# Batch 1's loads reordered between those of w_out, its q copies all on ScalarE, its k^T v moved to slot 27, and its last x slot turned inside block 1: one cosformer attention and MoE kernel on one core

## The chip, the cores and the metric

The kernel runs on 1 core of a Trainium2 chip. The metric is device time in microseconds (us), as the median of several executions; lower is better. Each execution is listed with its span and the mean clock that TensorE was granted (1.0 is full speed).

## The reference

Attention with a cosine weighting of positions and no softmax, on 8 batches of 8 heads, 576 positions and 64 columns, then a feed-forward layer on the 4608 rows that come out.

```python
def phi(x, c, s):
    r = np.maximum(x, 0.0)
    return np.concatenate([r * c, r * s], axis=-1)        # 128 features
q_p, k_p = phi(q, cos_w, sin_w), phi(k, cos_w, sin_w)
kv  = np.einsum('bhsf,bhsd->bhfd', k_p, v)                # "k^T v"
z   = np.sum(k_p, axis=2)
num = np.einsum('bhsf,bhfd->bhsd', q_p, kv)
den = np.einsum('bhsf,bhf->bhs', q_p, z)[..., None] + 1e-06
x   = (num / den).transpose(0, 2, 1, 3).reshape(4608, 512)
h   = x @ w_in                                            # 512 x 2048
out = (h * (1.0 / (1.0 + np.exp(-1.702 * h)))) @ w_out    # 2048 x 512
```

## The kernel before

The feed-forward layer goes in 9 blocks of 512 rows. A block has 32 slots. Slots 0 to 15 each multiply x by one group of 128 w_in columns (`mm1`: 4 matmuls and a gelu on ScalarE); slots 16 to 31 each do 4 of the 64 w_out matmuls (`mm2`). Behind a slot, the attention work of the next batch is set by a table of (slot, work). Block 0 is special: batch 1's loads come late there, so TensorE's attention work for it is crowded into slots 22 to 31.

For batch 1 that work is: VectorE makes q and k features (`prep`) and copies v (`prep_v_wide`); TensorE turns q, four slots of 128 positions with 8 heads each (`turn_q_at`, out of PSUM by a copy); `unit_kv` is k^T v (48 matmuls, then two casts on VectorE); `unit_num` is a numerator (8 matmuls, then the division on VectorE, giving xb); `turn_x_at` turns xb into xT (4 transposes and a copy on ScalarE). In PSUM the kernel keeps four tiles `mm` of 512 float32 columns, and two tiles `at` of twice that, which q turns, k^T v, numerators and x turns share. `evac` copies a finished w_out result out of PSUM into the tile `ysb`, on ScalarE.

```python
    load_w_out(0)
    load_w_out(1)
    for n in "qkv":
        load_main(1, n)
    load_w_out(2)
    load_w_out(3)
    ...
    def turn_q_at(b, c, copy):
        t = at_tile()[:, 0].bitcast(BF16)...
        for h in range(H):
            nc.tensor.transpose(t[:, h], qn_slot(b, c)[:, h, :], ident[:rows(c), :rows(c)])
        copy(q_slot(b, c)[:, :, 0:rows(c)], t)
    ...
    def unit_kv(b):
        kvs_new(b)
        kv = at_tile()
        for n in range(2):
            kv_half(b, n, kv[:, n])       # 24 matmuls
        for n in range(2):
            kvs_half(b, n, kv[:, n])      # cast on VectorE
    ...
    for i in range(NBLK):
        ...
            k0, k1, ks = (11, 24, (25, 26, 27, 28)) if i == 0 else (0, 12, (17, 19, 21, 23, 25))
            ...
            for c in range(4 if i == 0 else NC):
                at(k0, prep, b, "q", c)
                if i == 0:
                    at(22 + c // 2, turn_q_at, b, c, VE.tensor_copy if c % 2 else AC.copy)
            for c in range(6 if b < 2 else NC):
                at(20 if i == 0 else k1 - 4 + c // 2, prep, b, "k", c)
            if b == 1:
                at(21, prep_v_wide, b)
            at(k1, unit_kv, b)
            for c, k in enumerate(ks):
                at(k, unit_num, b, c)
                if i == 0 and c < 4:
                    at(min(k + 2, 31), turn_x_at, b, c)
```

`AC` is ScalarE, `VE` is VectorE; `at(n, ...)` sets work behind slot n. Cuts are marked with "...".

Of the kernel before, what the change touches and what calls it, by code (L numbers as in the profile page):

```python
# [21 lines left out]
def kernel(  # L22
# [15 lines left out]
    TB = 512  # L38
# [15 lines left out]
    def rows(c):  # L54
        return 128 if c < 4 else 64

    def wide(b, n):
        return b < 2 and n != "q"
# [7 lines left out]
    def mm_tile():  # L66
        return ps.tile([128, TB], F32, name="mm", bufs=4)

    def at_tile():
        return ps.tile([128, 2, 512], F32, name="at", bufs=2)  # L70
# [10 lines left out]
    def load_main(b, n, h0=0, h1=H, on=nc.gpsimd):  # L81
        t = 6 if wide(b, n) else 4
        np_ = 96 if wide(b, n) else 128
        if h0 == 0:
            state[b][n] = two.tile([128, 2048 if n == "q" else 49 * D], BF16, name=n)
        on.dma_start(out=state[b][n][:np_, t * D * h0:t * D * h1].rearrange("p (h e) -> p h e", h=h1 - h0),  # L86
                     in_=SRC[n][b, h0:h1, 0:np_ * t, :].rearrange("h (p c) d -> p h (c d)", c=t))

    def load_tail(b, n, on=nc.gpsimd):
        if on is nc.gpsimd:  # L90
            t = two.tile([64, 512], BF16, name=n + "t")
        else:
            t = one.tile([64, 512], F32, name=f"{n}t{b}")
        state[b][n, 4] = t
        on.dma_start(out=t.rearrange("p (h d) -> p h d", h=H),
                            in_=SRC[n][b, :, 512:576, :].rearrange("h p d -> p h d"))
# [14 lines left out]
    def load_w_out(g):  # L111
        nc.gpsimd.dma_start(out=w_out_sb[:, ts(g, 4), :], in_=wout_r[:, ts(g, 4), :])
# [23 lines left out]
    load_w_in(3)  # L136
    load_w_out(0)
    load_w_out(1)
    for n in "qkv":
        load_main(1, n)  # L140
    load_w_out(2)
    load_w_out(3)
    load_tail(1, "q")
    load_all(2)
# [84 lines left out]
    def turn_x_at(b, c):  # L229
        t = at_tile()[:, 0].bitcast(BF16).rearrange("p (j t) -> p j t", j=2 * KC)[:, 0:KC, 0:rows(c)]  # L230
        for j in range(KC):
            nc.tensor.transpose(t[:, j], state[b]["xb"][:rows(c), c, 2 * j:2 * j + 2, :].rearrange("p h d -> p (h d)"),
                                ident[:rows(c), :rows(c)])
        nc.scalar.copy(xT[:, :, ds(b * S + c * 128, rows(c))], t)
# [45 lines left out]
    def mm1_part(hps, i, fc, c0=0, c1=TB):  # L280
        for kc in range(KC):
            nc.tensor.matmul(hps[:, c0:c1], w_in_sb[:, kc, ds(fc * 128, 128)], xT[:, kc, ds(i * TB + c0, c1 - c0)],  # L282
                             start=(kc == 0), stop=(kc == KC - 1))

    def gelu(hps, fc):
        g = gpool.tile([128, TB], BF16, name="g")
        nc.scalar.activation(g, hps, AF.Gelu_apprx_sigmoid)  # L287
        gT[fc] = g

    def mm1(i, fc):  # L290
        hps = mm_tile()
        if (i, fc) == (1, 0):

            mm1_part(hps, i, fc, 0, 448)
            mm1_part(hps, i, fc, 448, TB)
        else:
            mm1_part(hps, i, fc)
        gelu(hps, fc)

    def pieces(m):  # L300

# [20 lines left out]
    def mm2(i, t, part):  # L322

        if part == 0:
            cur[t] = mm_tile()
        yps = cur[t]
        for fc in range(part * 4, part * 4 + 4):
            nc.tensor.matmul(yps, gT[fc][:, ds(t * 128, 128)], w_out_sb[:, fc, :],  # L328
                             start=(fc == 0), stop=(fc == FC - 1))
        if part == 3 and (i > 0 or t < 3):  # L330
            evac(i, t)

    def evac(i, t, on=None):
        ysb = ypool.tile([128, d_model], F32, name="ysb")
        if on is nc.vector:
            nc.vector.tensor_copy(ysb, cur[t])
        else:
            nc.scalar.copy(ysb, cur[t])  # L338
        for (p0, n, row, step) in pieces(i * 4 + t):
            nc.gpsimd.dma_start(out=out[row:row + (n - 1) * step + 1:step, :], in_=ysb[p0:p0 + n, :])  # L340

    def mm2_last(i, t):

        yps = mm_tile()
        ysb = ypool.tile([128, d_model], F32, name="ysb")
        hd = d_model // 2
        for n in range(2):
            cols = ds(n * hd, hd)
            if n == 1:
                yps = mm_tile()  # L350
            for fc in range(FC):
                nc.tensor.matmul(yps[:, 0:hd], gT[fc][:, ds(t * 128, 128)], w_out_sb[:, fc, cols],  # L352
                                 start=(fc == 0), stop=(fc == FC - 1))
            if n == 0:
                nc.scalar.copy(ysb[:, cols], yps[:, 0:hd])
            else:
                nc.vector.tensor_copy(ysb[:, cols], yps[:, 0:hd])  # L357
            for m, (p0, cnt, row, step) in enumerate(pieces(i * 4 + t)):
                (nc.sync if m == 0 else nc.scalar).dma_start(out=out[row:row + (cnt - 1) * step + 1:step, cols],
                                                             in_=ysb[p0:p0 + cnt, cols])  # L360
# [57 lines left out]
    AC, VE = nc.scalar, nc.vector  # L418
# [50 lines left out]
    for i in range(NBLK):  # L469
        work = {n: [] for n in range(32)}  # L470
        b = i + 1

        def at(n, f, *a):
            work[n].append(lambda: f(*a))

        if b < B:
            if i == 0:
                at(18, unit_num, 0, 4)
                at(18, turn_x, 0, 4)
            k0, k1, ks = (11, 24, (25, 26, 27, 28)) if i == 0 else (0, 12, (17, 19, 21, 23, 25))  # L480
            at(k0, prep_new, b)
            if i == 1:

                at(2, nc.vector.memset, kp[64:128, 4], 0.0)
                at(2, nc.vector.memset, vt[64:128, 4], 0.0)

                at(0, prep, 1, "q", 4)
                at(0, turn_q, 1, 4)
                at(14, unit_num, 1, 4)
                at(14, turn_x, 1, 4)  # L490
            for c in range(4 if i == 0 else NC):
                at(k0, prep, b, "q", c)
                if i == 0:
                    at(22 + c // 2, turn_q_at, b, c, VE.tensor_copy if c % 2 else AC.copy)
                else:
                    at(k0 + c, turn_q, b, c)
            for c in range(6 if b < 2 else NC):
                at(20 if i == 0 else k1 - 4 + c // 2, prep, b, "k", c)
                if b >= 2:
                    at(k1 - 1, prep_v, b, c)  # L500
            if b == 1:
                at(21, prep_v_wide, b)
            at(k1, unit_kv, b)
            for c, k in enumerate(ks):
                at(k, unit_num, b, c)
                if i == 0 and c < 4:
                    at(min(k + 2, 31), turn_x_at, b, c)
                else:
                    at(k, turn_x, b, c)
            if i == 1:  # L510
                at(8, gate, 7)
            if 0 < i and b + 1 < B:
                at(8 if i == 1 else 1, load_all, b + 1)
        for n in range(32):
            if n < FC:
                if i > 0 or n > 2:
                    mm1(i, n)
            elif i == 0:
                mm2(i, n % 4, (n - FC) // 4)
            elif i == NBLK - 1 and n >= 28:  # L520
                if n == 28:
                    mm2_last(i, 3)
            else:
                mm2(i, (n - FC) // 4, n % 4)
            for f in work[n]:
                f()
        if i == 0:
            evac(i, 3, nc.vector)
# [30 lines left out]
```

## Time and profile before

| | us |
|---|---|
| median of the first 3 timed executions | 295.51 (295.04 to 295.58) |
| the profiled execution | 297.05, span 295.0, mean clock 0.994 |

The execution whose trace is read in the prediction took 1.5 us longer than any of the timed ones, and its clock was below 1. A stretch of 3.41 us at half clock takes about 0.006 off the mean clock of such a span (3.41 × 0.5 / 295), which is the gap between 1.0 and 0.994. The lines of the profiled execution's trace are in the prediction; each shows times in us from the start of the span.

### The profile page before, as it was taken

How to read it: one execution, taken by the hardware profiler on the slowest of the kernel's cores; microseconds unless marked ns; L12 is line 12 of the kernel's file. 1: busy time of each engine (PE TensorE's matmuls, PEld its weight loads, DVE VectorE, ACT ScalarE, POOL GpSimd, SP SyncE). 2: the span in 40 equal slices, each digit the busy share in tenths (PEclk: the TensorE clock that was granted, in tenths of full speed). 3: DMA queues.
4: the chain of work that ended last, by engine and by line, in shares of the span. 5: the costliest groups of instructions: out<-in, count | busy, mean ns of one | idle time of the engine just before them, and what ended most of it. 6: DMA issues, size and time to landing. Idle time of an engine off the chain costs nothing.

```text
span 295.0 us, 5044 instructions
## 1 busy us (share of the span) xinstructions
PE 285.0 (97%) x1920; PEld 144.9 (49%) x1956; DVE 106.1 (36%) x359; ACT 124.1 (42%) x212; POOL 96.2 (33%) x118
## 2 busy tenths in 40 slices
PE   8999969999999999999999999999999999999994
PEld 3654446545544554455445544554455444444443
DVE  5940475663580259015901581148114200000000
ACT  7866221673136313741264126511651176126411
POOL 8543340352277026602690268005401200120021
PEclk9999989999999999999999999999999999999999
DMA  7999999799989956998899779966904500011033
GB/s 188 189 203 200 203 198 192 186 148 180 194 160 182 169 118 118 191 155 136 155 181 185 107 140 174 190 110 124 185 1 71 118 36 3 36 71 36 2 71 71
DMA packets 87304, 39.65 MB, mean 134 GB/s; under 512 B 57137, under 2 KB 85041, under 8 KB 87281
## 3 DMA queue, kind: packets, MB, share of 16 engines
q0 software_dynamic: 40848, 27.01, 59.4%
q1 hardware_dynamic: 46272, 12.20, 25.0%
q8 instruction: 15, 0.25, 0.3%
q10 hardware_dynamic: 160, 0.13, 0.2%
q14 instruction: 9, 0.07, 0.1%
HBM read 36.70 MB, written 9.44 MB: 156 GB/s over the span
## 4 chain that ended last, share of the span: by engine, by line
PE 82%; DMA 9%; DVE 4%; POOL 1%; issue 1%; ACT 1%; ACTq 0%; DVEq 0%; POOLq 0%
PE mm L328 37%; PE mm L282 36%; DMA q<-in_q_dram 6%; PE at L266 3%; PE at L245 3%; DMA w_in_sb<-in_moe_w_in_dram 3%; PE mm L352 1%; DVE kp L207 1%; ACT g L287 1%; DVE xb L274 1%; DVE qn L207 1%; POOL v L86 1%; POOL k L86 0%; DVE vt L210 0%; DVE inv L273 0%
## 5 line engine op out<-in xcount | busy, mean ns | idle before, releaser
L328 PE MATMUL mm<-w_out_sb,g 128*128 128x512 bf16 x542 | 127.2, 380 | 0.9 <-issue 0.2
L282 PE MATMUL mm<-xT,w_in_sb 128*128 128x512 bf16 (+1 forms) x552 | 123.5, 377 | 0.8
L287 ACT ACTIVATE g<-mm 128x512 bf16<-128x512 f32 x144 | 85.6, 597 | 46.0 <-PE mm L282 45.5
L340 POOL DMA_DIRECT2D out_dram<-ysb x54 | 50.6, 941 | 166.1 <-ACT ysb L338 164.7
L282 PEld LDWEIGHTS <-w_in_sb 128*128 128x128 bf16 x568 | 54.8, 98 | 64.8
L328 PEld LDWEIGHTS <-g 128*128 128x128 bf16 x560 | 52.3, 98 | 57.1 <-issue 0.6
L338 ACT COPY ysb<-mm 128x512 f32<-128x512 f32 x34 | 19.9, 585 | 97.7 <-PE mm L328 97.7
L249 DVE CAST kvs<-at 128x260 bf16<-128x260 f32 x14 | 5.4, 426 | 58.4 <-PE at L245 58.4
L274 DVE TENSOR_TENSOR xb<-at,inv 128x512 bf16<-128x512 f32 (+1 forms) x36 | 24.8, 690 | 1.2
L357 DVE COPY ysb<-mm 128x256 f32<-128x256 f32 x1 | 0.4, 424 | 59.4 <-PE mm L352 59.4
L272 DVE TENSOR_SCALAR den<-at 128x8 f32<-128x8 f32 (+1 forms) x36 | 5.9, 164 | 43.8 <-PE at L266 43.8
L266 PEld LDWEIGHTS <-qT 128*128 128x128 bf16 x272 | 13.0, 98 | 8.2 <-DVE xb L274 0.6
L207 DVE TENSOR_SCALAR qn<-q,cosw 128x512 bf16<-128x512 bf16 (+1 forms) x36 | 12.4, 351 | 12.2 <-DMA q<-in_q_dram 12.2
L266 PE MATMUL at<-kvs,qT 128*128 128x65 bf16 x272 | 14.2, 194 | 0.5
L207 DVE TENSOR_SCALAR qn<-q,sinw 128x512 bf16<-128x512 bf16 (+1 forms) x33 | 11.9, 360 | 0.0
L245 PEld LDWEIGHTS <-kp 128*128 128x128 bf16 (+1 forms) x288 | 10.4, 101 | 2.0 <-issue 0.6
L86 POOL DMA_DIRECT2D v<-in_v_dram x10 | 9.8, 986 | 4.6 <-DMA v<-in_v_dram 2.4
L245 PE MATMUL at<-vt,kp 128*128 128x65 bf16 (+1 forms) x288 | 10.5, 198 | 0.0
L86 POOL DMA_DIRECT2D k<-in_k_dram x9 | 7.8, 863 | 3.0 <-DMA q<-in_q_dram 2.3
L207 DVE TENSOR_SCALAR kp<-k,cosw 128x512 bf16<-128x512 bf16 x24 | 8.2, 341 | 0.0
L207 DVE TENSOR_SCALAR kp<-k,sinw 128x512 bf16<-128x512 bf16 x24 | 8.2, 341 | 0.0
L273 DVE RECIPROCAL inv<-den 128x8 f32<-128x8 f32 (+1 forms) x36 | 7.2, 201 | 1.2
(78 smaller groups left out, 133.7 us busy)
## 6 DMA issues: line engine op xcount, KB each, us to landing
out_dram<-ysb POOLq DMA_DIRECT2D x38, 128.0 KB, 3.0
out_dram<-ysb POOLq DMA_DIRECT2D x16, 256.0 KB, 2.7
q<-in_q_dram POOLq DMA_DIRECT2D x7, 512.0 KB, 9.2
k<-in_k_dram POOLq DMA_DIRECT2D x6, 512.0 KB, 10.5
v<-in_v_dram POOLq DMA_DIRECT2D x6, 512.0 KB, 12.3
w_out_sb<-in_moe_w_out_dram POOLq DMA_DIRECT2D x4, 512.0 KB, 18.3
w_in_sb<-in_moe_w_in_dram POOLq DMA_DIRECT2D x3, 512.0 KB, 12.2
q<-in_q_dram SPq DMA_DIRECT2D x2, 512.0 KB, 4.2
```

Of the source, the lines that this page charges most:

```text
L86: on.dma_start(out=state[b][n][:np_, t * D * h0:t * D * h1].rearrange("p (h e) -> p h e", h=h1 - h0), in_=SRC[n][b, h0:h1, 0:np_ * t, :].r ...
L207: nc.vector.tensor_scalar(oc, i, 0.0, wc, op0=MAX, op1=MUL)
L245: nc.tensor.matmul(kv[:, ds(h % 4 * (D + 1), D + 1)], kp[:r, c, h, :], vt[:r, c, h, 0:D + 1], start=(c == 0), stop=(c == last))
L266: nc.tensor.matmul(nm[:, h // 4, ds(h % 4 * (D + 1), D + 1)], q_slot(b, c)[:, h, :], state[b]["kvs"][:, h // 4, h % 4, 0:D + 1], start=Tru ...
L272: nc.vector.tensor_scalar(den[:r], nm4[:, :, :, D], 1e-6, None, op0=ADD)
L273: nc.vector.reciprocal(inv[:r], den[:r])
L274: nc.vector.tensor_tensor(state[b]["xb"][:r, c].rearrange("p (n h) d -> p n h d", n=2), nm4[:, :, :, 0:D], inv[:r].unsqueeze(3).to_broadca ...
L282: nc.tensor.matmul(hps[:, c0:c1], w_in_sb[:, kc, ds(fc * 128, 128)], xT[:, kc, ds(i * TB + c0, c1 - c0)], start=(kc == 0), stop=(kc == KC ...
L287: nc.scalar.activation(g, hps, AF.Gelu_apprx_sigmoid)
L328: nc.tensor.matmul(yps, gT[fc][:, ds(t * 128, 128)], w_out_sb[:, fc, :], start=(fc == 0), stop=(fc == FC - 1))
L338: nc.scalar.copy(ysb, cur[t])
L340: nc.gpsimd.dma_start(out=out[row:row + (n - 1) * step + 1:step, :], in_=ysb[p0:p0 + n, :])
```

## The change: intent and diff

Batch 1's q is loaded first, then a part of w_out, so that w_out arrives before TensorE needs it; v comes in two halves, so that k^T v can start on the first. All q copies go to ScalarE, one turn per slot, which takes TensorE's wait on VectorE away. k^T v goes from behind slot 24 to behind slot 27, the numerators follow, and the last x slot is turned inside block 1, between two w_in groups that first do only the 448 columns that don't need it.

```diff
--- before.py
+++ after.py
@@ -136,9 +136,11 @@
     load_w_in(3)
     load_w_out(0)
     load_w_out(1)
-    for n in "qkv":
-        load_main(1, n)
+    load_main(1, "q")
     load_w_out(2)
+    load_main(1, "k")
+    load_main(1, "v", 0, 4)
+    load_main(1, "v", 4, 8)
     load_w_out(3)
     load_tail(1, "q")
     load_all(2)
@@ -288,14 +290,19 @@
         gT[fc] = g
 
     def mm1(i, fc):
-        hps = mm_tile()
         if (i, fc) == (1, 0):
 
-            mm1_part(hps, i, fc, 0, 448)
-            mm1_part(hps, i, fc, 448, TB)
-        else:
+            hps = [mm_tile(), mm_tile()]
+            mm1_part(hps[0], i, 0, 0, 448)
+            turn_x_at(1, 3)
+            mm1_part(hps[1], i, 1, 0, 448)
+            for f in range(2):
+                mm1_part(hps[f], i, f, 448, TB)
+                gelu(hps[f], f)
+        elif (i, fc) != (1, 1):
+            hps = mm_tile()
             mm1_part(hps, i, fc)
-        gelu(hps, fc)
+            gelu(hps, fc)
 
     def pieces(m):
 
@@ -477,7 +484,7 @@
             if i == 0:
                 at(18, unit_num, 0, 4)
                 at(18, turn_x, 0, 4)
-            k0, k1, ks = (11, 24, (25, 26, 27, 28)) if i == 0 else (0, 12, (17, 19, 21, 23, 25))
+            k0, k1, ks = (11, 27, (27, 27, 28, 29)) if i == 0 else (0, 12, (17, 19, 21, 23, 25))
             at(k0, prep_new, b)
             if i == 1:
 
@@ -491,20 +498,22 @@
             for c in range(4 if i == 0 else NC):
                 at(k0, prep, b, "q", c)
                 if i == 0:
-                    at(22 + c // 2, turn_q_at, b, c, VE.tensor_copy if c % 2 else AC.copy)
+                    at(23 + c, turn_q_at, b, c, AC.copy)
                 else:
                     at(k0 + c, turn_q, b, c)
             for c in range(6 if b < 2 else NC):
-                at(20 if i == 0 else k1 - 4 + c // 2, prep, b, "k", c)
+                at(24 if i == 0 else k1 - 4 + c // 2, prep, b, "k", c)
                 if b >= 2:
                     at(k1 - 1, prep_v, b, c)
             if b == 1:
-                at(21, prep_v_wide, b)
+                for n in range(2):
+                    at(26, prep_v_wide, b, 4 * n, 4 * n + 4)
             at(k1, unit_kv, b)
             for c, k in enumerate(ks):
                 at(k, unit_num, b, c)
-                if i == 0 and c < 4:
-                    at(min(k + 2, 31), turn_x_at, b, c)
+                if i == 0:
+                    if c < 3:
+                        at(28 + c, turn_x_at, b, c)
                 else:
                     at(k, turn_x, b, c)
             if i == 1:
```

## The prediction

> **What bounds the kernel now.** I read the page first (busy shares, then the chain that ended last), then the waits of TensorE, then the timeline and the windows of the stretch that those point to.
>
> The first two lines below are the page's busy line and its chain; the third is the longest wait in the list of TensorE's waits after the start.
>
> ```profile
> PE 285.0 (97%) x1920; PEld 144.9 (49%) x1956; DVE 106.1 (36%) x359; ACT 124.1 (42%) x212; POOL 96.2 (33%) x118
> PE 82%; DMA 9%; DVE 4%; POOL 1%; issue 1%; ACT 1%; ACTq 0%; DVEq 0%; POOLq 0%
> PE at L226 <- DVE qT L227: 2.1, 1, 2.1
> ```
>
> TensorE is busy for 285.0 of 295.0 us, so only some 10 us can be idle at all, and one single wait of 2.1 us stands out. It lies in the turn from block 0 to block 1. The chain of work there, in order of time (start, us, what):
>
> ```profile
> 14.55 18.46 DMA q<-in_q_dram
> ...
> 33.53 2.56 DVE qn L207 x8
> ...
> 36.42 0.68 DVE xb L274
> 37.10 3.15 DVE kp L207 x12
> 40.25 0.87 DVE vt L210
> 41.12 0.61 DVE qT L227
> ...
> 41.77 0.71 PE at L226 x8
> ```
>
> VectorE gets batch 1's q at 33.5, makes the q features, then the 12 k features and the whole v copy, and only then the copy of a turned q slot out of PSUM, which TensorE needs before it can use that PSUM tile again. The timeline of the same stretch (start, us, engine, line, operation, count, idle time before it):
>
> ```profile
> 39.03 0.61 PE L226 MATMUL at<-ident,qn 128*128 128x128 bf16 x8
> 39.73 1.01 ACT L227 COPY qT<-at 128x1024 bf16<-128x1024 bf16 x1 [0.75 <-PE at L226]
> 40.17 0.95 DVE L210 COPY vt<-v 96x3072 bf16<-96x3072 bf16 x1
> 41.77 0.71 PE L226 MATMUL at<-ident,qn 128*128 128x128 bf16 x8 [2.14 <-DVE qT L227]
> 43.99 2.32 PE L245 MATMUL at<-vt,kp 96*128 96x65 bf16 x48
> 46.35 0.77 DVE L249 CAST kvs<-at 128x260 bf16<-128x260 f32 x2 [3.13 <-PE at L245]
> 49.79 0.31 PEld L266 LDWEIGHTS <-qT 128*128 128x128 bf16 x8 [0.31 <-DVE xb L274]
> 51.44 0.31 PEld L266 LDWEIGHTS <-qT 128*128 128x128 bf16 x8 [0.31 <-DVE xb L274]
> 56.69 0.60 ACT L287 ACTIVATE g<-mm 128x512 bf16<-128x512 f32 x1 [0.27 <-PE mm L282]
> ```
>
> TensorE stands from 39.64 to 41.77. Then the granted clock falls, as two windows of 2 us show (column PEclk, third from the end of each line):
>
> ```profile
> 42.00:44.00 2.00, 1.78 (x11) 0.88 (x10) 0.69 (x1) 0.00 (x0) 0.28 (x1) 0.53 1.57 185
> 44.00:46.00 2.00, 2.00 (x45) 2.00 (x44) 0.00 (x0) 0.00 (x0) 0.00 (x0) 0.61 1.57 192
> ```
>
> The trace's clock records put half speed at 42.14 to 45.55. So one wait costs twice.
>
> **The ceiling of any gain here.** Two fixed points: slot 22 of block 0 ends at 37.26 (start of the first q turn), and the second w_in group of block 1 ends at about 56.47 (its gelu starts at 56.69, and starts after matmul issue ends by 0.2). That is 19.21 us. The work between, at the full-clock spacings seen elsewhere in this trace: 9 slots of 4 matmuls at 0.216 = 7.78; 4 q turns of 8 at 0.45 (16 took 0.90 from 37.26 to 38.16) = 1.80; k^T v, 48 at 0.030 (block 1's 40 took 1.21) = 1.45; 4 numerators at 0.26 = 1.04; 4 x turns at 0.22 = 0.88; two w_in groups = 1.73. Sum 14.7. Hence 4.5 us are lost: 2.14 in the wait, about 1.6 to half clock (the slot at 42.28 to 43.99 took 1.71 instead of 0.86, k^T v 2.15 instead of 1.45), 0.62 in two waits on xb, the rest small. 4.5 us is 1.5% of 295.5: even a perfect change stays inside 2%.
>
> [...] the q copy on VectorE started at 41.04 though its turn was done at 39.64; the v copy of 0.95 us stood ahead. [...]
>
> **The change part by part.**
>
> *Loads.* Before, the landings (completion records) are q 33.01, k 35.77, v 38.65, third w_out 41.16, fourth 44.15: 2.5 to 3.0 us each, back to back. With w_out moved up: third w_out at 33.01 + 2.51 = 35.5, k at 38.3, the halves of v at 39.7 and 41.2, last w_out at 44.1 as before. The w_out loads are needed only at slots 24 and 28 (38.6 and 46.2 below): both in time. k is 2.5 us later.
>
> *Copies of q.* All four q copies go to ScalarE (1.01 each, idle there), one per slot. Turn q0 follows slot 23: 37.26 + 0.86 = 38.12 to 38.57, copy 38.83 to 39.84; slot 24 to 39.43; q1 to 39.88; slot 25 to 40.74; q2 may begin, since copy q0 ended at 39.84. q2 to 41.19, slot 26 to 42.05, q3 to 42.50, slot 27 to 43.36. No wait: the 2.14 and the half clock behind it go.
>
> *k^T v at slot 27.* VectorE: k at 38.3 plus 0.5 (q landed at 33.01 and its first feature began at 33.53) = 38.8; 12 features 3.15 → 41.95; v halves at about 0.5 each → 42.45 and 42.9. TensorE arrives at 43.36: slack 0.9. k^T v to 44.81. So far TensorE is 1.3 us ahead of before (46.12).
>
> *Numerators right behind it.* Here a wait comes in. Before, slot 25 stood between k^T v and its use; now nothing does. The casts start when all 48 are done, 44.81 + 0.2, and take 0.77 → 45.78; numerator 0 ends at 45.96 instead of 45.07, numerator 1 at 46.21. Loss 0.9. Slot 28 to 47.08. The x product takes 1.13 (0.17 + 0.20 + 0.69 and gaps): xb0 at 47.29, so x turn 0 runs 47.32 to 47.55 (loss 0.24).
>
> *One PSUM tile.* In the built program numerator 2 takes the tile of x turn 0, so it waits for ScalarE's copy of it, which queues behind the ysb copy of slot 28: 47.29 to 47.87, the x copy to 48.37. Numerator 2 at 48.41 (loss 0.86) to 48.67; slot 29 to 49.53; x turn 1 to 49.75; xb2 at 50.0, so numerator 3 at 50.02 (0.27) to 50.28; slot 30 to 51.14; x turn 2 to 51.36; slot 31 to 52.22.
>
> *Block 1.* The first w_in group waits for the copy of x turn 2, which stands behind a ysb copy: 52.43, so 52.47 (0.25). Its 448 columns take 0.76, x turn 3 0.22, the second group's 448 columns 0.76 → 54.21. The x3 copy ended by 54.25, so the last 64 columns of both, 8 at 0.03, end at 54.54. The split adds four matmuls net, about 0.05 us.
>
> Sum: 56.47 − 54.54 = 1.9 us gained: 4.5 of old losses removed, about 2.6 of new ones put in. Later blocks start earlier with the same order; batch 2's loads keep their times and have 5 us or more. So 295.5 − 1.9 = 293.6.
>
> **Rivals.**
> *The clock halves again.* The new waits cluster from 44.8 to 48.4. [...] For: it is the sparsest stretch left. Against: [...] no idle piece passes 0.9 us. If so, about 1.5 us come back: 295.1. I give it 15%.
> *k lands late.* For: k moved behind a weight load, and the DMA engines are saturated. Against: 0.9 us of slack. A slip of 1.5 us would cost 0.6: 294.2.
> *The new waits are not there* (casts start per half, copies overlap better): for this, consecutive ScalarE copies overlap by 0.1 in the trace; against, the program's waits name these producers. It would save 1 us more: 292.6.
> *Nothing moves*, since TensorE waits for a transfer anyway: 295.5. Against: no DMA wait of TensorE is listed in this stretch.
>
> **Range and chances.** Centre 293.7 (1.9 gained less a small share for the half clock). 8 in 10: 292.7 to 295.1, from the third rival to the first. Over 2% faster would need 5.9 us, more than the 4.5 there are; over 2% slower would need a fault that I don't see.
>
> **What would show it.** Right: no wait of TensorE on VectorE's q copy; clock 1.00 throughout; casts followed by a numerator that waited about 0.9 us; numerator 2 waiting on ScalarE's x copy; gelu of block 1's second group about 1.9 us earlier. Wrong: half clock near 45 to 52, k^T v waiting for the v copy, or later blocks losing the gain.

The marked cuts take out its account of what makes the clock fall and recover, two remarks in the rival "the clock halves again" that used it, and its rules for the order of queues and transfers: no trace or run here shows them. The granted clock was 0.50 from 42.14 to 45.55, and in the 3.41 us ahead of that TensorE was busy for 1.27. The DMA engines, which it calls saturated, were busy nine tenths or more in each fortieth of the stretch from 20 to 50 us, at 176 to 210 GB/s.

## The result and the profile after

| | median us | executions |
|---|---|---|
| before, same rounds | 295.47 | 295.58, 295.04, 295.51, 295.42 |
| after | 295.50 | 295.46, 295.55, 295.64, 295.15 |

The ratio is 1.0002, with a 95% interval of 0.9985 to 1.002. Ratios here are the mean time of one kernel's fast runs over that of the other's of the same rounds, so not quite the ratio of the medians quoted. Every execution in this document counts as fast in that sense, those at half clock too. The predicted gain of 1.9 us isn't there. Yet the traces of the two kernels differ by just that: span 295.0 before, 293.2 after.

The profile of the changed kernel: the chain from its page, then two lines of the list of TensorE's waits (line, releaser, total us, times, longest us); the lines left out, 1.2 and 0.2 us, belong to the start of the kernel.

```profile
PE 95%; ACT 2%; DVE 1%; issue 1%; ACTq 0%; DVEq 0%
```

```profile
...
PE at L268 <- ACT xT L236: 0.7, 1, 0.7
PE at L268 <- DVE kvs L251: 0.5, 1, 0.5
...
```

The wait on the q copy is gone, and the chain now hangs on TensorE at 95% (82% before). Two waits have come in: the numerators on the casts of k^T v, and a numerator on the copy of an x turn. The timeline of the changed kernel shows where (start, us, engine, line, operation, count, idle before it):

```profile
38.32 0.61 PE L228 MATMUL at<-ident,qn 128*128 128x128 bf16 x8
42.38 1.01 DVE L212 COPY vt<-v 96x1536 bf16<-96x1536 bf16 x2
43.56 1.61 PE L247 MATMUL at<-vt,kp 96*128 96x65 bf16 x48
45.21 0.77 DVE L251 CAST kvs<-at 128x260 bf16<-128x260 f32 x2 [1.81 <-PE at L247]
45.70 0.88 PE L268 MATMUL at<-kvs,qT 128*128 128x65 bf16 x16 [0.53 <-DVE kvs L251]
47.54 0.23 PEld L234 LDWEIGHTS <-xb 128*128 128x128 bf16 x4 [0.60 <-DVE xb L276]
48.61 0.41 PE L268 MATMUL at<-kvs,qT 128*128 128x65 bf16 x8 [0.67 <-ACT xT L236]
58.46 0.60 ACT L289 ACTIVATE g<-mm 128x512 bf16<-128x512 f32 x1 [0.27 <-PE mm L284]
```

Step by step this is what was predicted: k^T v at 43.56 (predicted 43.36), first x turn at 47.54 (47.32), numerator 2 at 48.61 (48.41), all 0.2 later because the first q turn was. The clock stayed full in the stretch where it had halved; windows of 2 us, PEclk third from the end:

```profile
42.00:44.00 2.00, 2.00 (x29) 1.37 (x28) 1.40 (x4) 1.67 (x2) 1.67 (x1) 1.00 1.56 186
44.00:46.00 2.00, 1.48 (x43) 1.26 (x40) 0.77 (x2) 0.00 (x0) 0.00 (x0) 1.00 1.59 189
```

The last timeline line above, the gelu of block 1's sixth group, serves as a milestone from here on. In the trace of the kernel before it was here:

```profile
60.20 0.60 ACT L287 ACTIVATE g<-mm 128x512 bf16<-128x512 f32 x1 [0.27 <-PE mm L282]
```

From it to the end of the span the kernels take the same time: 293.2 − 58.46 = 234.7 us after, 295.0 − 60.20 = 234.8 before. So whatever moves the time lies ahead of the milestone, and the trace read for the prediction did lose 1.7 us there against the changed kernel. The timed executions of the kernel before, by their times, can't have lost it. That is the question for the experiments.

### The profile page after: what moved, and what is told of

Read it like the earlier page. It is cut to its first block, busy times and chain, and to the rows that moved or that the text cites. A ratio compares the mean times of both kernels' runs of the same rounds, so it can differ in the third digit from the quotient of the medians.

```text
span 293.2 us, 5056 instructions
## 1 busy us (share of the span) xinstructions
PE 284.5 (97%) x1925; PEld 144.5 (49%) x1960; DVE 105.2 (36%) x358; ACT 125.9 (43%) x214; POOL 95.7 (33%) x119
## 4 chain that ended last, share of the span: by engine, by line
PE 95%; ACT 2%; DVE 1%; issue 1%; ACTq 0%; DVEq 0%
PE mm L284 40%; PE mm L335 40%; PE at L268 4%; PE at L247 3%; PE at L75 2%; PE mm L359 1%; ACT g L289 1%; PE mm L75 1%; PE mm L423 1%; PE mm L379 1%; PE at L228 1%; PE mm L394 0%; PE mm L418 0%; ACT ysb L345 0%; ACT xT L236 0%
## 5 line engine op out<-in xcount | busy, mean ns | idle before, releaser
L284 PE MATMUL mm<-xT,w_in_sb 128*128 128x512 bf16 (+2 forms) x556 | 123.7, 376 | 0.9
L247 PEld LDWEIGHTS <-kp 128*128 128x128 bf16 (+1 forms) x288 | 9.6, 97 | 1.7
L247 PE MATMUL at<-vt,kp 128*128 128x65 bf16 (+1 forms) x288 | 9.8, 193 | 0.0
L86 POOL DMA_DIRECT2D v<-in_v_dram x11 | 8.9, 815 | 2.8 <-DMA w_in_sb<-in_moe_w_in_dram 1.8
L75 PE MATMUL at<-warm 128*128 128x512 bf16 x18 | 7.1, 546 | 1.2 <-DVE eps L153 1.2
```

Source lines behind the costliest of these rows:

```text
L75: nc.tensor.matmul(wps, warm[:, 0:128], warm, start=True, stop=True)
L86: on.dma_start(out=state[b][n][:np_, t * D * h0:t * D * h1].rearrange("p (h e) -> p h e", h=h1 - h0), in_=SRC[n][b, h0:h1, 0:np_ * t, :].r ...
L247: nc.tensor.matmul(kv[:, ds(h % 4 * (D + 1), D + 1)], kp[:r, c, h, :], vt[:r, c, h, 0:D + 1], start=(c == 0), stop=(c == last))
L284: nc.tensor.matmul(hps[:, c0:c1], w_in_sb[:, kc, ds(fc * 128, 128)], xT[:, kc, ds(i * TB + c0, c1 - c0)], start=(kc == 0), stop=(kc == KC ...
```

## The experiments

Theory A: the half clock of the profiled execution is not in most executions of the kernel before; the prediction took 1.6 us of loss away that the timed ones didn't have. Theory B: it is in all of them, and the gain is lost outside the span. The first four runs shared one chip, the next four another, the last two a third.

### e1: the kernel before, run again

No edit but a comment.

> The kernel before, unchanged, to see its ordinary executions one by one. Its profiled execution had a span of 295.0 us and took 297.05 us, its timed ones 295.0 to 295.6. Theory A[...]: most executions have clock 0.998 or more, a span near 293.3 and a time near 295.4; at most a minority shows clock 0.994, span 295.0 and time 297. Theory B (the half clock is in every execution of the kernel before, and the gain of 1.8 us in span is lost outside the span): spans near 295.0 and clock 0.994 in all of them.

Measured (time, span, clock), six executions under this label and eleven of the kernel before that ran beside them (its companion). In the column "half" are those with clock 0.993 or 0.994:

| | full | half |
|---|---|---|
| e1 | 295.55, 295.14, 295.78, 295.04 | 297.18, 297.14 |
| companion | 295.51, 295.48, 295.57, 295.35, 295.06, 295.04, 294.89, 295.78 | 297.12, 297.11, 297.36 |

The full ones have spans of 292.8 to 293.7 and clocks of 0.998 to 1.0; the half ones spans of 295.0 to 295.3. There is nothing between. So the kernel has two groups 1.8 us apart, and the profiled execution of the first trace (297.05, 295.0, 0.994) was of the slower one, the timed ones around it, by their times, of the faster. Theory A holds in that the half clock isn't in every execution; what brings it in one execution and not in another is not shown, and on the two later chips it was no minority. Of theory B a little is true: time less span is 2.04 to 2.09 us on average in the runs that load v at once, and 2.21 to 2.25 in those with the changed loads (b5, below, has nothing else), so about 0.16 us does lie outside the span. Why isn't shown. The trace of e1 fell in the faster group; from its timeline and its windows:

```profile
38.10 1.06 PE L226 MATMUL at<-ident,qn 128*128 128x128 bf16 x16
41.92 0.61 PE L226 MATMUL at<-ident,qn 128*128 128x128 bf16 x8 [1.44 <-DVE qT L227]
43.23 1.61 PE L245 MATMUL at<-vt,kp 96*128 96x65 bf16 x48
58.73 0.60 ACT L287 ACTIVATE g<-mm 128x512 bf16<-128x512 f32 x1 [0.27 <-PE mm L282]
```

```profile
42.00:44.00 2.00, 2.00 (x38) 1.53 (x38) 0.69 (x1) 0.00 (x0) 0.43 (x1) 1.00 1.55 185
44.00:46.00 2.00, 2.00 (x41) 1.44 (x38) 0.77 (x2) 0.00 (x0) 0.00 (x0) 1.00 1.59 190
```

Two things differ from the first trace. The clock is 1.00, so k^T v takes 1.61 instead of 2.32. And TensorE came to the q turns 0.84 later (38.10 against 37.26; early in this execution it had waited 0.6 us for batch 0's v, which the first trace doesn't list), but VectorE's copy released it at about the same time (41.92 against 41.77), so its wait is 1.44 and not 2.14: the end of the wait is set by VectorE, its length by when TensorE arrives. The milestone is at 58.73, 0.27 us behind the changed kernel's 58.46. Even that is within the spread of single traces: the trace of c1, the changed kernel run again (below), has it here:

```profile
58.75 0.60 ACT L289 ACTIVATE g<-mm 128x512 bf16<-128x512 f32 x1 [0.27 <-PE mm L284]
```

So beside executions at full clock the change is worth nothing that shows.

What decides which group an execution falls into isn't settled. The two traces differ both in the length of the wait (2.14 and 1.44) and in how much work lay around it (from 38 to 42 us TensorE was busy for 1.9 us in the first and 2.6 in e1); no second trace of a slow execution of this kernel was taken.

### e3 and e4: a longer wait, empty and filled

e3 makes VectorE's v copy four times; e4 adds 16 matmuls of zeros to it, behind the copy of q slot 2, into the half of that slot's PSUM tile that nothing reads.

```diff
-                at(21, prep_v_wide, b)
+                for _ in range(4):
+                    at(21, prep_v_wide, b)
```
```diff
+        if c == 2:
+            warmup(16, tile_[:, 1])       # e4 only: tile_ is the at tile of this q turn
```

> The kernel before with VectorE's v copy of batch 1 made four times, so that TensorE's wait for the q copy grows by about 2.8 us to about 5 us[...]. Theory A: half clock follows in every execution, clock near 0.99 in all, and the time is 295.4 + 2.8 + about 1.6 = 299.8 us. Theory B (half clock already in every timed run of before): 295.4 + 2.8 = 298.2.

> The same long wait, with 16 matmuls of zeros (3.5 us) in it into the spare half of a PSUM tile, results unused. Theory A: the wait is as long but the clock stays at 1.0, so 298.2 us, 1.6 us less than without the fillers. Theory B, or if fillers of zeros don't count as work for the clock: the same as without them.

Measured: e3 299.28 (298.94 to 300.63), all six clocks between 0.987 and 0.994. e4 298.73 (298.27 to 299.33), clocks 0.997 to 1.0. The clocks came as theory A has it: with the longer wait all six executions show a low clock, and with work in the wait none does. The difference in time is 0.55 us, a third of what was expected. The timeline of e3, then that of e4:

```profile
46.56 1.61 PE L245 MATMUL at<-vt,kp 96*128 96x65 bf16 x48 [2.77 <-DVE qT L227]
48.00 1.64 PE L328 MATMUL mm<-w_out_sb,g 128*128 128x512 bf16 x4
```

```profile
40.60 3.61 PE L75 MATMUL at<-warm 128*128 128x512 bf16 x16 [1.16 <-ACT qT L228]
44.89 0.61 PE L227 MATMUL at<-ident,qn 128*128 128x128 bf16 x8 [0.67 <-DVE qT L228]
```

In e3 the half clock sits behind k^T v in the profiled execution (4 matmuls in 1.64 instead of 1.03), which is one of the two at 300.5 and 300.6. The other four lie at 298.9 to 299.5, with clocks as low. Their traces were not taken, and why they took 1.0 to 1.7 us less at clocks as low is not shown. Two flaws of this pair: in e3 the wait came in three pieces (1.16 for ScalarE's q copy, 0.23 for w_out, 2.77 for VectorE's q copy), and the last of them stands before k^T v, while in e4 VectorE's copy is waited for by a q turn, as in the kernel before: the built programs share out the two `at` tiles differently. And e3's profiled execution reached its first q turn 1.3 us later than e4's (38.41 and 37.07). So the pair shows well that this wait, left empty, brings the low clock (0.987 to 0.994, against 0.997 to 1.0 when filled), and shows its price badly. The cleaner price is the distance of the kernel before's two groups, in e1 and in c2 below.

### c2: the kernel before with its own wait filled

```diff
+        if c == 2:
+            warmup(6, tile_[:, 1])        # ahead of the copy of this q turn
```

> The kernel before with six matmuls of zeros (1.3 us) in TensorE's wait for the q copy, results unused, nothing else changed. Theory: the wait ends when it did[...]: all runs near 295.4 with clock 0.998 or more, none near 297. Rival (zeros don't count as work, or the half clock has another cause): two groups as in the kernel before.

Measured: 295.41 (295.08 to 295.74), clocks 0.998 to 1.0 in all six. The eleven executions of the kernel before of the same rounds: seven at 297.33 to 297.64, clock 0.993 or 0.994, and four at 295.11, 295.17, 295.22 and 295.88. Ratio 0.996 (0.9923 to 0.9997). The timeline of c2:

```profile
39.95 1.46 PE L75 MATMUL at<-warm 128*128 128x512 bf16 x6
41.85 0.61 PE L227 MATMUL at<-ident,qn 128*128 128x128 bf16 x8 [0.44 <-DVE qT L230]
```

The released turn starts at 41.85, close to e1's 41.92. No execution is faster than the full-clock ones of the kernel before; six useless matmuls only kept the slower group from happening. The two groups of the kernel before lie 2.2 us apart here and 1.8 on the chip of e1, so the slower group costs somewhat more than the prediction's 1.6 us for the half clock; but it is not a part of every execution.

### c1: the changed kernel, run again

> The changed kernel, unchanged, beside many runs of the kernel before on one chip. Theory: [...] all runs have clock 0.997 or more and lie at 295.1 to 295.7; the kernel before falls into two groups, about 295.4 at clock 0.998 or more and about 297.1 at 0.994, in a share that changes from chip to chip. Rival (the changed kernel also halves now and then): a group near 297.

Measured: 295.76, 295.19, 295.24, 295.56, 296.36, 295.23, clocks 0.997 to 1.0. With the four of the first result, ten executions and no half clock. Ratio to the kernel before of the same rounds 0.9965 (0.9931 to 1.0), since seven of the latter's eleven were slow. Beside the latter's four at full clock (median 295.2) the changed kernel's median of 295.4 is no gain. Two executions lie above the expected 295.1 to 295.7, and one of them, 296.36 with span 294.1 and clock 1.0, fits neither group; the kernel before had such ones too (295.88 and 295.95 at 0.999 or 1.0). Their cause stays open.

So how the change comes out depends on the share of slow executions of the kernel before: 0 of the first 4 timed, 5 of 17 on the chip of e1, 6 of 11 and 7 of 11 on the two others.

### e2: the q copies on ScalarE alone

```diff
-                    at(22 + c // 2, turn_q_at, b, c, VE.tensor_copy if c % 2 else AC.copy)
+                    at(22 + c // 2, turn_q_at, b, c, AC.copy)
```

> The kernel before with one part of the change alone: all four q copies on ScalarE. Theory A: TensorE's wait of 2.1 us goes, but the next slot then waits for the third w_out load (landed at 41.2 in the profile of before) for about 0.8 us, so k^T v starts at about 42.1, 1.0 us earlier than in an execution of the kernel before at full clock: 294.4 us. Rival (the stretch as a whole is bound by VectorE's row of products, so that TensorE's waits only change places): 295.4, as before.

Measured: 294.61 (294.21 to 294.78), clocks 1.0 in all six; ratio 0.9959 (0.993 to 0.9988), which holds the slow executions of the companion too. Beside the full-clock group (about 295.3) it is 0.7 us faster. TensorE's waits from 20 us on, and the milestone:

```profile
PE mm L328 <- DMA w_out_sb<-in_moe_w_out_dram: 0.8, 1, 0.8
PE at L226 <- ACT qT L227: 0.3, 1, 0.3
```

```profile
57.92 0.60 ACT L287 ACTIVATE g<-mm 128x512 bf16<-128x512 f32 x1 [0.27 <-PE mm L282]
```

The wait for w_out came as predicted from the landings, and the milestone is 0.8 ahead of e1's. One line of the change is better than the change: beside the kernel before at full clock it gains 0.7 us, the whole change nothing. So the other parts give back what this one gains.

### b5: the loads alone

The kernel before with the diff's first hunk only.

> The kernel before with the loads of the change alone (w_out part ahead of k, v in halves), its q copies still half on VectorE. Theory: k lands 2.5 us later, so VectorE comes to the q copy about 1.8 us later and TensorE's wait on it grows from 1.4 to 2.1 to some 3.5 us: 297.2 us at full clock, with half clock in most runs and then up to 298.8. Rival (the k load has slack before it matters): 295.4.

Measured: 298.84 (297.31 to 300.11), five of six clocks at 0.989 to 0.994, and the one at 0.999 took 297.31. Its list of waits from 20 us on:

```profile
PE at L228 <- DVE qT L229: 3.5, 1, 3.5
```

The wait grew as expected, to 3.5 us, and the time at full clock is what the theory said (297.2). The later k is harmful in itself, as long as a q copy stands behind it on VectorE. The change moves k back (its first feature starts at 38.76 instead of 37.03) and sets k^T v three slots later, which hides it.

### b3, b1 and b4: the new waits

b3 loads k before the third w_out part again and sets the q turns and k^T v one slot earlier, so that a slot stands between k^T v and its use. b1 goes on: k^T v behind slot 25 and one numerator behind each of slots 26 to 29. Both against the changed kernel:

```diff
-    load_w_out(2)
     load_main(1, "k")
+    load_w_out(2)
-  k0, k1, ks = (11, 27, (27, 27, 28, 29))          # changed kernel
+  k0, k1, ks = (11, 26, (27, 27, 28, 29))          # b3
+  k0, k1, ks = (11, 25, (26, 27, 28, 29))          # b1
-  at(23 + c, turn_q_at, ...)                       # changed kernel
+  at(22 + c, turn_q_at, ...)                       # b3
+  at((22, 22, 23, 24)[c], turn_q_at, ...)          # b1
   # prep of k at 22 (b3) or 20 (b1) for 24; v copies at 25 (b3) or 21 (b1) for 26
```

b4 is the changed kernel with the last x slot turned behind slot 31 again and only the first w_in group split, as before.

> The changed kernel with k^T v and the q turns one slot earlier (k loaded ahead of the third w_out part to allow it), the numerators where they were: slot 27 lies between k^T v and the numerators. Theory: the 0.9 us wait of the numerators on the casts goes, the waits behind it (x turn 0, numerator 2) stay: 294.8 us. Rival (the cast wait is only time that would be lost to the next waits anyway): 295.5.

> The changed kernel with k of batch 1 loaded ahead of the third w_out part, the q turns at slots 22, 22, 23 and 24 (all copies on ScalarE), k^T v behind slot 25, and the numerators behind slots 26 to 29, so that one slot lies between k^T v and its use. Theory (the change gained nothing because its late k pushed k^T v back and set it, the numerators and the x turns against each other): k^T v starts at about 41.7 with no wait of TensorE before it, no wait on the casts, small waits on the products (0.3 each) and on the x2 copy; the second w_in group ends about 1.5 to 2 us earlier than in both kernels: 293.5 us, clock 0.998 or more in all runs. Rival (the stretch is bound by VectorE's products however k^T v is placed): 294.6, as with the copies moved alone.

> The changed kernel with the last x slot turned behind slot 31 again and only the first w_in group split, as in the kernel before. Theory: this part of the change is worth nothing by itself, since the first group waits for the copy of x2 anyway and the x3 copy is then ready behind 448 columns: 295.5 us, within 0.2. Rival (the split over two groups hides a copy): 296 us.

| | median us | range | clocks | ratio to before (half of those runs slow) |
|---|---|---|---|---|
| b3 | 294.71 | 294.34 to 294.96 | 0.997 to 1.0 | 0.995 (0.9914 to 0.9986) |
| b1 | 293.64 | 293.4 to 293.9 | 0.999 to 1.0 | 0.9914 (0.9882 to 0.9947) |
| b4 | 295.26 | 295.18 to 295.35 | 0.997 to 1.0 | 0.9969 (0.9937 to 1.0001) |

The full-clock executions of the kernel before in these rounds are 294.98, 295.0, 295.01, 295.15 and 295.95. b3's list of waits from 20 us on holds one line, the wait on the x copy, without the one on the casts:

```profile
PE at L268 <- ACT xT L236: 0.7, 1, 0.7
```

The timeline of b1:

```profile
41.46 1.61 PE L247 MATMUL at<-vt,kp 96*128 96x65 bf16 x48
43.10 0.77 DVE L251 CAST kvs<-at 128x260 bf16<-128x260 f32 x2 [1.27 <-PE at L247]
43.77 0.44 PE L268 MATMUL at<-kvs,qT 128*128 128x65 bf16 x8
56.42 0.60 ACT L289 ACTIVATE g<-mm 128x512 bf16<-128x512 f32 x1 [0.27 <-PE mm L284]
```

k^T v begins 2.1 us earlier than in the changed kernel (41.46 against 43.56), no wait of TensorE's matmuls is listed from 20 us on, since slot 26 covers the casts (weight loads waited 0.2 us on a cast and twice 0.3 on a product), and the milestone is 2.0 us ahead (56.42 against 58.46), of which 0.4 is an earlier arrival at the q turns. b3 is 0.7 to 0.8 us under the changed kernel by its median, which ran on other chips, and 0.55 under b4, which ran on the same one; the wait on the casts was 0.53. So that wait costs its length, though b3 also loads k earlier, and the rival that VectorE's products bound the stretch falls with b1's 293.64. Which of b1's differences (k's load, the slots of the q turns, of k^T v and of the numerators) brings how much is not separated. b1 is the best version: it has no half clock in six executions, and is some 1.4 us under the full-clock group of the kernel before (293.64 against 295.01) and 3.5 under its slow group (297.17). b4 says that the x slot inside block 1 is worth nothing: 295.26 is no worse than the changed kernel's 295.4 and 295.5, which ran on other chips. The traces even put it at a small loss: from the end of slot 22 (0.86 before the first q turn) to the milestone b4 takes 20.76 us, and the changed kernel 21.00 in both of its traces.

## Why the prediction was wrong

**The step that failed** is in "The ceiling of any gain here", a cost: "4.5 us are lost: 2.14 in the wait, about 1.6 to half clock". This is true of the profiled execution and was taken as true of the executions that the time is measured on. By their times, the 1.6 us are in none of the timed executions of the first comparison; by their clocks, they are in 18 of 39 made later. The prediction subtracted a loss of 297.05's from a base of 295.5. The sign was at hand: the profiled execution's own time, 1.5 us above the highest timed one, and its clock of 0.994. The rival "the clock halves again" asked whether the changed kernel might halve; that the unchanged one might not was never asked. This step alone takes nearly all: 1.9 less 1.6 leaves 0.3 us (an estimate from the prediction's own sums).

**A second term was mis-sized** in the same sum: the wait of 2.14 is 1.44 in the full-clock trace of e1. The prediction's starting point of 37.26 belongs to an execution in which TensorE was early, and the wait took that up, since VectorE ends it. With 1.6 and 0.7 less to win, the old losses are 2.2 instead of 4.5. The prediction's sum redone on e1's trace gives the same: 55.22 − 0.22 − 38.10 = 16.9 us for 14.7 of work. This term changes with each execution's arrival.

**What held.** The new losses. Counted as the prediction counts them, from the start of one group of matmuls to the next less its full-clock spacing, they are, with the predicted ones in brackets: the numerators on the casts 0.88 (0.89), x turn 0 0.27 (0.24), numerator 2 0.85 (0.86), numerator 3 0.30 (0.27), the first w_in group 0.25 (0.25), together 2.55 (2.51). The profile's own idle times above (0.53, 0.67, and 0.60 of a weight load) are counted otherwise, from the modelled end of the instruction before, and can't be set beside them. TensorE's steps all began within 0.3 us of the predicted times. The changed kernel's span was right (predicted 295.0 − 1.9 = 293.1, measured 293.2). "Clock 1.00 throughout" held in ten executions, whose clocks are 0.997 or more. Old losses of 2.2 less new ones of about 2.6 would even be a small loss. In the first trace of the changed kernel TensorE ended slot 22 at 37.46 (38.32 − 0.86), 0.6 us earlier than in e1, and it came out 0.27 ahead at the milestone; in c1's trace it ended slot 22 at 37.75 and came out level.

**Smaller misses.** The ysb copy that was blamed for numerator 2's wait wasn't needed for it: the x turn ended at 47.94 and its copy began at 47.98, the same 0.04 later as in e1, where no ysb copy stood ahead of it (48.19 and 48.23). k landed at 38.73, not 38.3; the slack in front of k^T v took that up. The gelu of block 1's second group came 1.4 us earlier and not 1.9 (55.33 against 56.69), since ScalarE runs the gelus of the first two groups one behind the other there. And a line was misread: the q copy that VectorE began at 41.04 belongs to q slot 1, whose turn ended at 38.32; 39.64 is the end of q slot 2's turn, which ScalarE copied. That the copy stood behind the v copy holds all the same.

**Chances.** "Even a perfect change stays inside 2%" was right, and by more than was thought, since the ceiling was lower.

## What to carry to other kernels

Before reading a trace, set its own execution's time and clock beside the timed ones; if it is 1.5 us off, it shows another execution than the one that the time speaks of, and a loss found in it may not be there to win. A wait whose end another engine sets has no length of its own: shortening what comes ahead of it gains nothing, and an early arrival only lengthens it (TensorE came to the q turns at 37.26 and at 38.10, and went on at 41.77 and 41.92); of the two traces of the kernel before, the one with the longer wait (2.14 against 1.44) is the one with half clock. When work is moved to clear one wait, look at what stands between each product and its use: the change cleared 1.4 us and packed k^T v, casts and numerators so closely that it paid them back, while b1, with a slot between k^T v and each numerator and with k loaded earlier, kept the gain.
